# Centring the first half of a weight matrix on three visits of the second attention instead of in the first

## The chip, the cores and the metric

One core of a Trainium2 chip runs the whole program. The metric is the device time of one execution in microseconds (us). Three runs of the kernel before took 1073.25, 1074.12 and 1074.61 us; their median is 1074.12.

## The reference

Attention with a hashed mask (a query sees only keys of its own bucket), then a Fourier mixing block with a residual, a layer norm and a two-layer perceptron. Cut to what matters:

```python
# attention: B, H, S, D = 4, 8, 768, 64; bits of q and k give buckets, mask = same bucket
attn = softmax(where(mask, q @ k.T / sqrt(D), -1e9)) @ v
x = attn.transpose(0, 2, 1, 3).reshape(B, S, H * D)
u = x + real(fft(fft(x, axis=1), axis=2))
un = (u - mean(u, -1)) / sqrt(var(u, -1) + 1e-06)
out = u + maximum(un @ w_ch1, 0.0) @ w_ch2      # w_ch1: 512 x 2048, w_ch2: 2048 x 512
```

The kernel does not subtract the mean of `u` from each row. It subtracts from `w_ch1` the mean of each of its columns, once, which gives the same product: then a constant added to a row of `u` adds nothing. The division by the standard deviation comes after the second layer.

## The kernel before, in words

**Order.** The batch has four items. The second to fourth attentions run beside the mixing block of the item before them. In all attentions a *visit* is one block of 128 keys of one pair of heads: `attention(b)` yields once a visit, 24 times (4 pairs of heads by `NT` = 6 blocks). The first attention (`b` = 0) runs beside the arrival of `w1`, the on-chip copy of `w_ch1` (128 partitions by 4 row blocks by 2048 columns). That part stands in `tc.manual_schedule`: each engine's queue has the order in which the program writes it. From the second attention on, a planner in the tile framework orders each queue by priorities, by when it reckons operands and buffers ready, and by ties that the program gives: `in_turn()` (L683) queues what it encloses behind the last exponential or copy noted for ScalarE and the last operation noted for VectorE (`done_by`), `behind()` (L879) gives matmuls of the attention more priority.

**A visit of the attention** (`n` counts pairs of heads, `c` key blocks). `scores` (L886): on TensorE the mask (L898) and the scores (L909), half by half, into the PSUM tiles `sc`, of which there are two; the exponential `pk` on ScalarE (L922), in one of two buffers. `tally` (L1027): VectorE adds the exponentials up (`acc`, L1041). `finish` (L1003): `values` (L942), 8 matmuls L947, of the visit before; at the last blocks the key sums (`sum`, L957), and `scale` (L963) with copies on ScalarE (L968, L971, L990) and small steps on VectorE (L979 to L997). `prepare(n + 1)` is advanced by one step a visit: transposes (L779), norms on ScalarE (L761), bits by matmul (L812, L838) and thresholds on VectorE (L816 to L828).

**Arrival of w1** (`weights1`, L722). It comes in 16 slices of 128 by 512, as 64-bit numbers, by DMAs on SP's queue (L704), seven ahead; a slice is fetched into a raw buffer after the conversion that empties that buffer. Slice `i` is row block `i % 4` of the column block `i // 4`. `narrow` converts one: VectorE L639, L643, L649; ScalarE L647, L654, L655. The first attention calls the arrival on four visits of five (L1586), one slice a call.

**Means** (`average`, L659, and `centre`, L675). `average(f)` sums the columns of a column block of 512: 8 matmul instructions into the PSUM tile `ws` (L664), a copy to SBUF on ScalarE (`part`, L669), and at its second step the matmul `wm` (L672, 2 instructions), which gives every partition the mean. `centre` subtracts it from the four row blocks on VectorE (L678). The tiles `ws` and `wm` come from `pt` (L520): tag `ps`, two buffers once `roomy` is off, shared with the bits, the key sums and most tiles of the mixing block. Before, the arrival does this for the first two column blocks: one call after the block's last slice the sums, on the call after that the mean and the subtractions, each ahead of that call's slice or between slices. For the last two blocks the sums and means come after the first attention (L1594 to L1599), are copied to SBUF, and are subtracted on visit 2 of the second attention (L1612).

**Beside the second attention** the mixing of item 0 runs (`mix(0)`), with 2 steps ahead of the visits and then enough steps a visit to keep in pace (L1615): `fold` (VectorE, L1122 to L1140), the channel transform (`cs`, L1162), the sequence transform, 4 steps of pairs of PSUM tiles A and B (L1191), which VectorE adds to `x` (L1205), then `mlp7`, a seven-product form of the perceptron. Its first use of `w1` is `quarters(0)` (L1257): sums and differences of quarters of `w1` on VectorE (L1264 to L1267) and writes of blocks of `w1` to DRAM on SP's queue (L1269), from where items 1 to 3 read them back (L1444). By the pace, `quarters(0)` belongs to visit 7.

Of the kernel before, what the change touches and what calls it, by code (L numbers as in the profile page):

```python
# [24 lines left out]
DFF = 4 * DM  # L25
# [5 lines left out]
NDC = DM // P  # L31
GTT = 2
GT = GTT * P
WC = 512
# [451 lines left out]
def _main(  # L486
# [172 lines left out]
    def average(f):  # L659


        ps = pt([P, WC], f"ws{f}")
        for c in range(NDC):
            nc.tensor.matmul(  # L664
                ps[32 * c : 32 * c + 32, :], ones, w1[:, c, f : f + WC],
                start=True, stop=True,
            )
        part = wt([P, WC], F32, "u", f"part{f}", 2)
        nc.scalar.copy(part, ps)  # L669
        yield  # L670
        ps = pt([P, WC], f"wm{f}")
        nc.tensor.matmul(ps, mean, part, start=True, stop=True)  # L672
        yield ps

    def centre(f, avg):  # L675
        for c in range(NDC):
            w = w1[:, c, f : f + WC]
            nc.vector.tensor_tensor(w, w, avg, op=ALU.subtract)  # L678

    ET = mybir.EngineType  # L680
    done_by = {}

    @contextmanager  # L683
    def in_turn():

        with ExitStack() as st:
            for ins in done_by.values():
                st.enter_context(tc.issue_after(ins.ins))
            yield
# [32 lines left out]
    def weights1():  # L722
        slices = [
            (w1[:, c, f : f + WC], moe_w_ch1[c * P : (c + 1) * P, f : f + WC])
            for f in range(0, DFF, WC)
            for c in range(NDC)
        ]
        zt = wt([P, 3, 2 * WC], F32, "z", "zraw1", 1)
        ft = wt([P, 12, WC], F32, "F", "fraw", 1)
        raws = [zt[:, i] for i in range(3)] + [  # L730
            ft[:, i : i + 2].rearrange("p i w -> p (i w)") for i in range(0, 8, 2)
        ]
        arrival = Arrival(slices, raws, 0, nc.sync)
        for i in range(arrival.depth):
            arrival.fetch(i)
            if i == 2:
                load(1)
        yield
        half = None
        for i in range(len(slices)):  # L740
            arrival.convert(i, ft[:, 8 + i % 4].bitcast(I32))
            yield
            if half:
                centre(half[0], next(half[1]))
                half = None
            if i % NDC == NDC - 1:


                f = i // NDC * WC
                if f < DFF // 2:  # L750
                    half = f, average(f)
                    next(half[1])


    xs = {}
# [164 lines left out]
    def weights(pk, g, ps):  # L920

        done_by[ET.Activation] = nc.scalar.activation(  # L922
            pk[:, g, :, 0:HALF], ps[:, :, 0:HALF], AF.Exp, scale=SCALE
        )

    def weigh(n, c, pss):
# [6 lines left out]
        if kb is not None:  # L933
            for h in range(2):
                w = pk[:, :, h, 0:HALF]
                done_by[ET.DVE] = nc.vector.scalar_tensor_tensor(  # L936
                    w, qb[:, h].rearrange("p (g s) -> p g s", g=2), kb[:, h, c : c + 1], w,
# [61 lines left out]
    def attention(b):  # L999
# [14 lines left out]
        for t in range(NPAIR):  # L1014
# [12 lines left out]
            def tally(c, pk, sums):  # L1027
# [10 lines left out]
                else:  # L1038

                    for g in (0, 1) if b == 0 else (slice(0, 2),):  # L1040
                        done_by[ET.DVE] = nc.vector.tensor_tensor(  # L1041
                            acc[:, g], (first if c == 1 else acc)[:, g], new[:, g],
# [102 lines left out]
    def mix(b):  # L1145
# [8 lines left out]
        for par in range(2):  # L1154
            for t in range(NT // 2):
# [12 lines left out]
                for k in kinds:  # L1168
                    done_by[ET.Activation] = nc.scalar.copy(
                        f[:, k, k : hd + 1 - k],  # L1170
# [14 lines left out]
        for j in range(NDC):  # L1185
# [10 lines left out]
            for ps, op in (pa, ALU.add), (pb, ALU.subtract):  # L1196
                for i in range(2):
# [4 lines left out]
                    else:  # L1202
                        f = ps[:, HW : HALF + 1]
                        f = bass.AP(f.tensor, f.offset, [f.ap[0], [HW, 2], [-1, HW]])
                    done_by[ET.DVE] = nc.vector.tensor_tensor(  # L1205
                        u, u, f, op=op if (j < 2) ^ i else ALU.add
# [371 lines left out]
    with tc.manual_schedule(engines={ET.PE, ET.DVE, ET.Activation, ET.Pool, ET.SP}):  # L1578
        for _ in prepare(0):
            pass  # L1580
        roomy[0] = False
        for i, _ in enumerate(attention(0)):
            if i == 2 * NT - 1:
                nc.sync.dma_start(ch, cn["ch"].ap())
                nc.sync.dma_start(sq, cn["sq"].ap())
            if i % 5 < 4:  # L1586
                next(other, None)
        for _ in other:
            pass
        pwf = wt([P, 2, P], F32, "ef", "pwf", 1)  # L1590
        nc.sync.dma_start(pwf, cn["pw"].ap())
        nc.scalar.copy(pw, pwf)
        means = []
        late = [(f, average(f)) for f in range(DFF // 2, DFF, WC)]  # L1594
        for _, avg in late:
            next(avg)
        for f, avg in late:
            means.append((f, wt([P, WC], F32, "u", f"mean{f}", 2)))
            nc.scalar.copy(means[-1][1], next(avg))  # L1599
    for b in range(B):  # L1600
        if b > 0:

            wait = 0
            if b == 1:
                next(other)
                next(other)
                wait = 2
            steps, done = NPAIR * NT - wait, 2 if b == 1 else 0  # L1610
            for i, _ in enumerate(attention(b), 1):
                if b == 1 and i == 2:  # L1612
                    for f, avg in means:
                        centre(f, avg)
                while done * steps < (MIX - LEFT) * (i - wait):  # L1615
                    next(other)
                    done += 1
        if b == B - 1:
            roomy[0] = True

            ms = const.tile([P, 3], F32, tag="ms", name="ms")
            nc.vector.tensor_reduce(ms[:, 0:2], norms, axis=AX.X, op=ALU.max)
            nc.vector.tensor_reduce(ms[:, 2:3], strange, axis=AX.X, op=ALU.max)
            ps = pt([1, 3, P], "norms_t")
            for io in range(3):
                nc.tensor.transpose(ps[:, io, :], ms[:, io : io + 1], ident)
            mt = const.tile([1, 5], F32, tag="mt", name="mt")
            nc.vector.tensor_reduce(mt[:, 0:3], ps, axis=AX.X, op=ALU.max)  # L1630
            nc.vector.tensor_tensor(mt[:, 3:4], mt[:, 0:1], mt[:, 1:2], op=ALU.mult)
            nc.vector.tensor_scalar(
                mt[:, 4:5], mt[:, 3:4], (SAFE / SCALE / 2) ** 2, None, op0=ALU.is_gt
            )
            fl = const.tile([1, 1], I32, tag="fl", name="fl")
            nc.vector.scalar_tensor_tensor(
                fl, mt[:, 2:3], 0.0, mt[:, 4:5], op0=ALU.is_gt, op1=ALU.max
            )
            large = nc.values_load(fl[0:1, 0:1], min_val=0, max_val=1)
        for _ in other:  # L1640
            pass
        other = mix(b)
        if b == 0:
            zt2 = wt([P, 3, 2 * WC], F32, "z", "zraw2", 1)
            arrival2 = weights2()
            other = after(NT, other, islice(arrival2, HF + 2))
# [47 lines left out]
```

## Time and profile before

| what | value |
|---|---|
| median of 3 runs | 1074.12 us |
| the profiled execution | 1074.1 us |
| its span | 1072.3 us |
| TensorE matmul, busy | 1033.3 us (96%) |
| VectorE, busy | 779.6 us (73%) |
| ScalarE, busy | 489.2 us (46%) |
| first attention | from about 13 to 113 us |
| sums, copies, means and subtractions of the first two column blocks | 33.5 to 43.0 us and 58.1 to 66.7 us |
| the same of the last two | 112.6 to 120 us; subtractions 119.7 to 131.3 us |
| writes of w1 to DRAM (24) | 6 from 91.8 us, 18 from 125.2 to 137.8 us |

The profile is of one execution. PE is TensorE, DVE VectorE, ACT ScalarE, POOL GpSimd, SP the queue that issues most DMAs; L664 is line 664 of the kernel. Times are in us from the start of the span. A row of the timeline or of a group gives the engine, the line, the operation, output and inputs by the program's names, and in brackets how long the engine sat idle ahead of it and what ended that. "The chain" is the work that ended last, followed back from the end. Rows by stretch give for each engine the busy time within the stretch and the number of instructions, then TensorE's granted clock, the share of the DMA engines and GB/s.

### The profile page before, as it was taken

Reading aid. Unit: us, or ns where it says so; the run is one execution under the profiler, and the core shown is the slowest. Engines: PE = TensorE matmul, PEld = TensorE weight load, DVE = VectorE, ACT = ScalarE, POOL = GpSimd, SP = SyncE. Lnnn points to the kernel's source line nnn. Section 1 sums busy time; section 2 is a strip of 40 time slices with the busy share of each in tenths; the row PEclk is TensorE's granted clock in tenths of the full one; section 3 lists DMA queues with packets and bytes.
Section 4 is the critical chain, followed back from the end, with each engine's and each line's share of the span. In section 5 each row is a group of like instructions: output and inputs, shape, how many; then the busy total and the mean of one; then the engine's idle time right before and its main releaser. Section 6 shows DMA issues by size and latency. Waiting matters only on the chain.

```text
span 1072.3 us, 14129 instructions
## 1 busy us (share of the span) xinstructions
PE 1033.3 (96%) x4965; PEld 632.4 (59%) x4965; DVE 779.6 (73%) x1326; ACT 489.2 (46%) x993; POOL 59.6 (6%) x132
## 2 busy tenths in 40 slices
PE   7999899999999999999999999999999999999996
PEld 3333364457644676546665675555675579668575
DVE  5789969996799967877758877767857885644353
ACT  7888564761386323455236315354325512440420
POOL 0000000011000020100000020010000012200000
PEclk9999999999999999999999999999999999999999
DMA  8754551470154451223072242322042204223301
GB/s 207 200 143 85 112 136 45 135 233 1 35 153 150 136 194 36 45 67 81 12 200 74 66 123 88 59 64 61 15 125 86 64 25 172 65 74 100 117 20 42
DMA packets 175711, 103.13 MB, mean 96 GB/s; under 512 B 129553, under 2 KB 162961, under 8 KB 175633
## 3 DMA queue, kind: packets, MB, share of 16 engines
q1 hardware_dynamic: 169840, 88.65, 30.7%
q0 software_dynamic: 4224, 13.11, 3.9%
q8 instruction: 41, 0.67, 0.3%
q10 hardware_dynamic: 1568, 0.39, 0.2%
q14 instruction: 38, 0.30, 0.1%
HBM read 81.14 MB, written 20.97 MB: 95 GB/s over the span
## 4 chain that ended last, share of the span: by engine, by line
PE 74%; DVE 14%; ACT 5%; issue 2%; DMA 2%; SPq 1%; DVEq 0%; ACTq 0%
PE o L1350 25%; PE h_p L1471 23%; PE oo L947 9%; PE sc L909 8%; PE cs L1162 3%; DVE pk L936 2%; DVE acc L1041 2%; ACT pk L922 2%; PE A L1191 2%; PE B L1191 1%; PE sum L957 1%; DMA kn<-in_k_dram 1%; DVE x L1205 1%; PE bits L838 1%; SPq L576 1%
## 5 line engine op out<-in xcount | busy, mean ns | idle before, releaser
L1350 PE MATMUL o<-w,h 128*128 128x256 f32 x1152 | 258.6, 381 | 0.9 <-DVE w L1362 0.5
L1350 PEld LDWEIGHTS o<-w,h 128*128 128x128 f32 x1152 | 216.7, 190 | 41.6 <-issue 6.4
L922 ACT ACTIVATE pk<-sc 128x768 f32<-128x768 f32 x192 | 147.4, 808 | 78.6 <-PE oo L947 35.5
L1471 PE MATMUL h_p<-x,w 128*128 128x384 f32 x448 | 164.5, 494 | 2.4 <-ACT w L1538 1.7
L936 DVE SCALAR_TENSOR_TENSOR pk<-qb,kb,pk 128x768 f32<-128x768 bf16 x132 | 128.8, 1012 | 39.4 <-ACT pk L922 39.3
L909 PE MATMUL sc<-qt,kt 64*128 64x384 f32 x768 | 153.6, 503 | 1.6 <-ACT pk L922 1.4
L947 PE MATMUL oo<-pk,vn 128*64 128x385 f32 (+1 forms) x768 | 146.2, 495 | 1.5 <-DVE pk L936 1.3
L1471 PEld LDWEIGHTS h_p<-x,w 128*128 128x128 f32 x448 | 81.9, 190 | 68.3 <-issue 9.3
L1471 PE MATMUL h_p<-w 128*128 128x384 f32 x288 | 105.9, 489 | 0.0
L1041 DVE TENSOR_TENSOR acc<-acc,pk 128x1536 f32<-128x1536 f32 (+1 forms) x64 | 98.5, 1550 | 5.4 <-ACT pk L922 5.2
L947 PEld LDWEIGHTS oo<-pk,vn 128*64 128x64 f32 x768 | 50.5, 136 | 86.5 <-issue 73.7
L909 PEld LDWEIGHTS sc<-qt,kt 64*128 64x128 f32 x768 | 66.2, 186 | 55.4 <-issue 19.3
L1471 PEld LDWEIGHTS h_p<-w 128*128 128x128 f32 x288 | 53.7, 190 | 38.8 <-issue 1.6
L1362 DVE SCALAR_TENSOR_TENSOR w<-o,rs,w 128x256 f32<-128x256 f32 x56 | 26.6, 480 | 41.6 <-PE o L1350 41.6
L1380 ACT COPY tq<-o 128x256 f32<-128x256 f32 x24 | 8.9, 372 | 104.0 <-PE o L1350 104.0
L1485 ACT ACTIVATE h<-h 128x384 f32<-128x384 f32 x72 | 37.4, 524 | 29.0 <-DVE h L1527 14.0
L1350 PE MATMUL o<-w 128*128 128x256 f32 x176 | 42.2, 383 | 0.3 <-DVE w L1362 0.2
L1522 DVE TENSOR_TENSOR h<-h 128x384 f32<-128x384 f32 x32 | 17.8, 555 | 29.2 <-ACT h L1521 29.1
L1100 POOL DMA_DIRECT2D out_dram<-w x30 | 16.3, 546 | 405.4 <-issue 321.4
L1350 PEld LDWEIGHTS o<-w 128*128 128x128 f32 x176 | 32.9, 190 | 7.6 <-DVE w L1362 1.2
L1396 DVE TENSOR_TENSOR tq<-tq,o 128x256 f32<-128x256 f32 x24 | 10.0, 418 | 36.4 <-PE o L1350 36.4
L1369 ACT COPY tq<-o 128x256 f32<-128x256 f32 x24 | 8.8, 368 | 60.3 <-PE o L1350 60.2
(171 smaller groups left out, 1306.0 us busy)
## 6 DMA issues: line engine op xcount, KB each, us to landing
w<-ad SPq DMA_DIRECT2D x168, 128.0 KB, 2.0
w<-bd SPq DMA_DIRECT2D x42, 512.0 KB, 4.5
zraw<-in_moe_w_ch_dram POOLq DMA_DIRECT2D x16, 512.0 KB, 3.9
bd<-w SPq DMA_DIRECT2D x14, 512.0 KB, 4.4
vn<-in_v_dram SPq DMA_DIRECT2D x32, 192.0 KB, 3.3
qn<-in_q_dram SPq DMA_DIRECT2D x120, 48.0 KB, 2.4
kn<-in_k_dram SPq DMA_DIRECT2D x60, 96.0 KB, 3.1
zraw<-in_moe_w_ch_dram SPq DMA_DIRECT2D x8, 512.0 KB, 6.6
```

The costliest lines, as they stand in the source:

```text
L909: last[0] = nc.tensor.matmul(ps[:, h, 0:HALF], kt[rows, ks], qt[rows, qs], start=kb is not None or early, stop=not early,)
L922: done_by[ET.Activation] = nc.scalar.activation(pk[:, g, :, 0:HALF], ps[:, :, 0:HALF], AF.Exp, scale=SCALE)
L936: done_by[ET.DVE] = nc.vector.scalar_tensor_tensor(w, qb[:, h].rearrange("p (g s) -> p g s", g=2), kb[:, h, c : c + 1], w, op0=ALU.is_equa ...
L947: oo = nc.tensor.matmul(oos[g][h * D : (h + 1) * D, 0:w], nat["v", n][:, (2 * c + h) * D : (2 * c + h + 1) * D], pk[:, g, h, 0:w], start=( ...
L1041: done_by[ET.DVE] = nc.vector.tensor_tensor(acc[:, g], (first if c == 1 else acc)[:, g], new[:, g], op=ALU.add,)
L1162: nc.tensor.matmul(ps[:, pc + 2 * lo : pc + 2 * hi - 1 : 2], z[:, cp, pc, par, t * P : (t + 1) * P], ch[:, cp, pc, lo:hi], start=(cp == 0) ...
L1191: nc.tensor.matmul(ps[:, cols], F[:, par, k, t, j * P : (j + 1) * P], sq[:, t, k, cols], start=(t == 0), stop=(t == 1),)
L1350: nc.tensor.matmul(ps, a[:, r], right7[i][:, r], start=start and r == 0, stop=r == HF // 2 - 1, skip_group_check=not start,)
L1362: nc.vector.scalar_tensor_tensor(t[:, cols], src, r, t[:, cols], op0=ALU.mult, op1=ALU.add)
L1471: nc.tensor.matmul(ps, left[:, k], right[i][:, k], start=start and k == 0, stop=k == 1, skip_group_check=not start,)
L1485: done_by[ET.Activation] = nc.scalar.activation(h, h, AF.Relu)
L1522: done_by[ET.DVE] = nc.vector.tensor_tensor(c22, c21, c22, op=ALU.add)
```

## The change

The arrival of `w1` no longer averages and centres anything. A new generator, `centrings`, does the first two column blocks: it lets four visits pass, makes the sums of block 0 on the fifth, its mean and subtractions and the sums of block 1 on the sixth, and the mean and subtractions of block 1 on the seventh. It is called once a visit of the second attention, ahead of that visit's steps of the mixing block, within `in_turn()`. The last two blocks stay as they were.

```diff
+    def centrings(columns, visits):
+
+        for _ in range(visits):
+            yield
+        for f in columns:
+            avg = average(f)
+            next(avg)
+            yield
+            centre(f, next(avg))
+        yield
+
...
-        half = None
         for i in range(len(slices)):
             arrival.convert(i, ft[:, 8 + i % 4].bitcast(I32))
             yield
-            if half:
-                centre(half[0], next(half[1]))
-                half = None
-            if i % NDC == NDC - 1:
-
-
-                f = i // NDC * WC
-                if f < DFF // 2:
-                    half = f, average(f)
-                    next(half[1])
...
+    centred = centrings(range(0, DFF // 2, WC), 4)
     for b in range(B):
...
                 if b == 1 and i == 2:
                     for f, avg in means:
                         centre(f, avg)
+                if b == 1:
+                    with in_turn():
+                        next(centred, None)
                 while done * steps < (MIX - LEFT) * (i - wait):
                     next(other)
                     done += 1
```

## The prediction, made before the result was known

> **What bounds the kernel now.** I read the page's slices first, then the busy time by stretch, then the timeline of the first attention, then the chain of waits.
>
> The slices, of 26.8 us each:
>
> ```profile
> PE   7999899999999999999999999999999999999996
> DVE  5789969996799967877758877767857885644353
> ACT  7888564761386323455236315354325512440420
> ```
>
> TensorE reads as full nearly everywhere, so the share cannot tell which stage is worth what. The busy time by stretch (length, then busy time of each engine) can:
>
> ```profile
> 46.00:58.00 12.00, 8.88 (x62) 3.45 (x58) 11.62 (x16) 8.91 (x17) 0.00 (x0) 1.00 0.66 174
> ...
> 119.00:131.00 12.00, 10.36 (x66) 4.86 (x66) 12.00 (x25) 6.54 (x12) 0.00 (x0) 1.00 0.55 120
> 131.00:166.00 35.00, 35.00 (x214) 21.08 (x213) 24.84 (x36) 19.26 (x39) 1.86 (x3) 1.00 0.52 121
> 166.00:184.00 18.00, 15.93 (x68) 8.18 (x67) 16.93 (x23) 8.72 (x18) 0.53 (x1) 1.00 0.18 59
> ```
>
> The reader is to see three regimes. In the first attention (about 13 to 113 us) VectorE and ScalarE limit and TensorE has holes: 3.1 us in 46 to 58. From 119 to 131 VectorE is full. From 131 to 166, where the visits of the second attention lie to which the change moves work, TensorE has no hole at all: 35.00 of 35.00.
>
> The timeline at the two averages of the first attention (start, length, what, idle time before it and who ended it):
>
> ```profile
> 33.82 1.04 PE L664 MATMUL ws<-w,ones 128*32 128x512 f32 x8
> ...
> 34.93 0.59 ACT L669 COPY part<-ws 128x512 f32<-128x512 f32 x1 [2.30 <-PE ws L664]
> ...
> 39.39 1.13 PE L672 MATMUL wm<-part,mean 128*128 128x512 f32 x2
> ...
> 40.57 2.46 DVE L678 TENSOR_TENSOR w<-w,wm 128x512 f32<-128x512 f32 x4
> ```
>
> ```profile
> 58.10 1.07 PE L664 MATMUL ws<-w,ones 128*32 128x512 f32 x8 [1.94 <-DVE qkb L816]
> ...
> 59.23 0.58 ACT L669 COPY part<-ws 128x512 f32<-128x512 f32 x1 [4.22 <-PE ws L664]
> ...
> 63.05 1.12 PE L672 MATMUL wm<-part,mean 128*128 128x512 f32 x2
> ...
> 64.21 2.48 DVE L678 TENSOR_TENSOR w<-w,wm 128x512 f32<-128x512 f32 x4 [1.81 <-PE wm L672]
> ```
>
> ScalarE stands still 2.30 and 4.22 us ahead of the copies of the sums (L669). The second time TensorE itself waits until VectorE has emptied the PSUM tile of the previous bits (L816). The chain of waits goes through these pieces:
>
> ```profile
> 40.65 2.38 DVE w L678 x4
> ...
> 58.10 1.11 PE ws L664 x8
> 59.21 0.02 issue
> 59.23 0.58 ACT part L669
> ```
>
> **What the Trainium skill says.** "PSUM — Partial Sum Buffer", Engine vs sequencer instructions: the queues of ScalarE and VectorE are strictly first in, first out, and matmuls start and complete in program order. The trace agrees: behind the copy waiting 4.22 us stands the conversion of slice 8 (L647), whose data had landed long before; it starts at 59.72. "Perfetto Trace Analysis", Identifying the Most-Contended Engine: matmul busy share is no good measure of nearness to the roofline. So I use it only where the chain also runs on TensorE; from 131.2 to 165.8 every piece of the chain is TensorE. "VectorE: DVE Perf Modes", Mode 1×: a two-tensor fp32 operation gives one result a cycle, also with a PSUM operand, at 0.96 GHz. For 512 columns that is an estimated 533 ns; the trace has 680 ns from PSUM (wm) and from SBUF (mean) alike, so reading the average in PSUM costs VectorE nothing extra.
>
> **The change, part by part.**
>
> *Removed from the first attention.* Twice: 8 sum matmuls (1.04 and 1.07), a copy (0.59 and 0.58), the averaging matmul (1.13 and 1.12), four subtractions (2.46 and 2.48). TensorE 4.36, ScalarE 1.17, VectorE 4.94 us. What this is worth I get by walking the engines' queues with the same durations.
>
> First average: the exponential of visit 5 ends at 32.63. Without the copy ScalarE does the conversion of slice 4 (0.68+0.69+0.77+0.18, 2.3 with gaps) and reaches the next exponential at 35.1 rather than 37.61; its scores follow the key sums on TensorE at 34.0, so they are there. ScalarE then has 1.5 exponential, 1.2 for the scaling copies and 2.2 conversion: the exponential of visit 7 at 40.0 rather than 42.27. Gain 2.3. VectorE gains more (no subtractions, 2.46), but must wait for that exponential.
>
> Second average: the exponential of visit 10 ends at 55.01, with the 2.3 taken off 52.7. Conversion of slice 8 until 54.9. The scores of visit 11 can follow the bits matmuls on TensorE at about 54.4, so its exponential starts at 55.2 rather than 61.91: gain 6.7. Then TensorE limits: values, key sums and scores (1.5+0.7+0.9) put the next exponential at 59.3 (was 65.45, gain 6.15), and values ahead of the scaling copies the one after at 64.5 (was 70.15). ScalarE is full again from there and the gain stays **5.6 us**. The loads of the fourth head pair shift with it: SP starts them at 63.35 only because its last fetch of w1 waits for the conversion of slice 8 (end 61.82). Bounds: 7.7 if all of both stalls and copies came off (2.30+0.59+4.22+0.58); 4.0 if VectorE, busy 11.62 of 12 us in 46 to 58, holds the walk back.
>
> *Added to the second attention.* The calls at visits 1 to 4 issue nothing. Visit 5 issues 8 sum matmuls and a copy; visit 6 the averaging matmul, four subtractions, then 8 sum matmuls and a copy; visit 7 the averaging matmul and four subtractions. By the scores in the timeline these visits begin near 136, 144 and 150 us. TensorE there has no hole, so its part is on the path: 2 x 1.05 + 2 x 1.12 = **4.3 us**. ScalarE's 1.17 lies in 15.7 us of idle time (131 to 166), VectorE's 4.94 in 10.2 us. If VectorE's cover were gone, its 4.94 would replace TensorE's 4.3, 0.6 more.
>
> *Waits added.* In the second attention the general PSUM tag ("ps") has two buffers. The sum tile holds one until its copy, the average tile one until the fourth subtraction, 2.5 us. Queued behind on TensorE are the pairs A and B (L1191), which need both; scores and values (1.49+1.44 us) have their own tiles and can go first if the planner puts them first. The trace of before shows no such overlap here. Bounds: +2.5 for each of two averages if nothing fits in between, that is +5; and below nothing, -4.0, because the sum matmuls need only w1 and a buffer and may be planned into the holes before and after (119 to 131: 1.64; 166 to 184: 2.07; together 3.7), plus little elsewhere. I take 0, between them: one visit's scores and values are as long as one holding.
>
> *In-turn.* The copies and subtractions stay behind the last noted exponential and accumulation. VectorE is idle from 143.28 to 146.34, so the first subtractions find room; behind the second stand L1205 and the quarters (L1264). Taken at 0, bounds 0 to +1.
>
> *SP and GpSimd.* Of the 24 writes of w1 to DRAM (L1269, 24 x 0.618 us of SP) 16 read the first two column blocks. Before, six went at 91.76 and 18 from 125.16 to 137.8. Now these 16 can go only after the subtractions, past about 150: 16 x 0.62 = 9.9 us of SP among the loads of the last pair of that batch (147.38 to 161.0). SP is then nearly free until 193.6, and the first read back stands at 193.61, so I cost it at nothing; without that cover it is the last rival below. The conversions' fetches on SP come earlier, as walked. GpSimd's queue has none of the moved work and only fetches of the second weight behind other engines: 0.
>
> *Unchanged.* The last two blocks' means and their eight subtractions (119.7 to 131.3).
>
> **Sum.** -5.6 + 4.3 + 0 = -1.3 us. Against the profiled execution (1074.1 us; span 1072.3 and 1.8 around it) that is 1072.8; the median of the runs shown is 1074.12, the same within 0.1, so 1072.8 stands for it too. What this kernel's measurement can tell from no change is about 0.2%, 2.1 us: faster means below 1072.0, slower above 1076.3.
>
> **Rivals.**
> *A, the trade above:* 1072.8, its own range 1072.0 to 1076.3. For it: TensorE's 35.00 of 35.00.
> *B, the added matmuls find cover.* The planner starts sums in TensorE's holes at 119 to 131 and the later ones at 166 to 184 shrink, 3.7 us in all; if half to nearly all of the 4.3 is covered, about 2.2 paid in the middle: 1074.1 - 5.6 + 2.2 = 1070.7. For it: such early issue is seen for loads and norms (the norm of the last keys at 165.95). Against it: cs matmuls ahead of the sums in order want the same buffers.
> *C, the PSUM buffers become the bound.* Place: L1191 at visits 6 and 7. Price: 2.5 us for each average and 1.1 for each sum whose copy is late, 7.2 at most. It decides the sign once over 1.3 + 2.1 = 3.4 us of it is exposed; all exposed gives 1074.1 - 1.3 + 7.2 = 1080.0, in the middle some 1077.5. Against it: scores and values fill.
> *D, SP's writes stand ahead of the last pair's loads* and wait for the subtractions. ScalarE's norm of those queries starts at 158.58, about 3 us after the last load (154.53 + 1.05) is issued, so a delay reaches the exponentials behind it. Price 9.9 less some 5 of slack: 1074.1 - 1.3 + 4.9 = 1077.7.
>
> **Chances.** A 0.42, B 0.41, C 0.12, D 0.05. So faster 0.41, same 0.42, slower 0.17. The range: 1069.0 (B with 0.5 of its cost paid) to 1077.0 (the lower part of C and D) leaves out some 0.05 below and 0.13 above.
>
> **What will show it.** Right: no ws, part or wm before 100 us except the late blocks'; the exponential that was at 70.15 at about 64.5; scores of the second attention's first visit near 110.1 rather than 115.69; TensorE full from about 126 to 165, with 16 sum and 4 averaging instructions more. Wrong: a gain under 4 at the end of the first attention (VectorE held the walk back), holes on TensorE before A and B (C), sums in the holes (B), or a ScalarE norm waiting for a load (D).

## The result and the profile after

The changed kernel takes **1078.06 us** (median of 6 runs, 1077.35 to 1078.51) against 1073.86 us for the kernel before beside it: ratio **1.0035** (95% interval 1.0024 to 1.0045), 3.8 us slower. The prediction was 1072.8 with 1069.0 to 1077.0. The profiled execution took 1077.4 us with a span of 1075.6 us (1072.3 before).

Busy time by stretch, kernel after:

```profile
46.00:58.00 12.00, 11.58 (x85) 4.42 (x84) 11.40 (x21) 11.81 (x21) 0.00 (x0) 1.00 0.43 136
119.00:131.00 12.00, 10.53 (x65) 5.16 (x62) 11.63 (x18) 5.27 (x11) 0.00 (x0) 1.00 0.32 87
131.00:166.00 35.00, 34.37 (x205) 19.48 (x205) 21.52 (x33) 16.79 (x33) 1.86 (x3) 1.00 0.44 109
166.00:184.00 18.00, 13.10 (x58) 6.98 (x57) 16.48 (x28) 7.84 (x16) 0.53 (x1) 1.00 0.39 118
```

The first attention did what was hoped: in 46 to 58 TensorE rose from 8.88 to 11.58 us. From 119 to 131 the hole is as large as before (10.53 of 12), so no added matmul went there. The stretch that got worse is the last: from 166 to 184 TensorE fell from 15.93 to 13.10 us busy. (The same stretch of time holds somewhat different work in the two kernels.)

I use the start of a visit's exponential (L922) as a landmark; visits are counted from 0 through both attentions, so visit 24 is the first of the second attention and visit 30 the first of its second head pair. After minus before, in us (the whole run after lies about 0.3 earlier from its start):

| visit | 7 | 11 | 12 | 13 | 16 | 24 | 28 | 29 | 30 | 31 | 32 | 35 | 95 |
|---|---|---|---|---|---|---|---|---|---|---|---|---|---|
| after | -2.67 | -7.47 | -7.06 | -6.85 | -3.60 | -4.55 | -5.84 | -2.88 | -2.52 | -3.63 | **+4.73** | +4.04 | +3.51 |

Two steps are not those of the prediction. The gain falls by 3.3 between visits 13 and 16, and **8.4 us are lost between visits 31 and 32**, of which 7.7 are left at visit 35. (A visit's start is a place in a planned order, not a sum of costs: e17 below starts visit 32 11.5 us later than the kernel before and visit 35 1.0 us earlier.) TensorE's timeline there, kernel after (start, length, engine, line, output and inputs, count, idle time before and who ended it):

```profile
144.78 1.12 PE L672 MATMUL wm<-part,mean 128*128 128x512 f32 x2
145.84 1.06 PE L664 MATMUL ws<-w,ones 128*32 128x512 f32 x8
146.83 1.56 PE L909 MATMUL sc<-qt,kt 64*128 64x384 f32 x8
148.32 1.51 PE L947 MATMUL oo<-pk,vn 128*64 128x385 f32 x8
149.77 0.92 PE L1191 MATMUL A<-sq,F 128*128 128x193 f32 x4
...
165.60 1.10 PE L672 MATMUL wm<-part,mean 128*128 128x512 f32 x2
166.54 1.47 PE L1191 MATMUL A<-sq,F 128*128 128x193 f32 x8
170.21 1.57 PE L1191 MATMUL B<-sq,F 128*128 128x193 f32 x8 [2.21 <-DVE w L678]
...
173.71 1.61 PE L909 MATMUL sc<-qt,kt 64*128 64x384 f32 x8 [1.60 <-ACT pk L922]
```

At the first average scores and values stand between `wm` and the first A, and TensorE does not wait: so far the prediction's picture. But these pairs A, B now come one visit later than before (149.77, was 147.66), and the second average, made at 165.60, falls behind the sums of the finished head pair (L957, 164.68). In this order only A stands between: the fourth B waits 2.21 us for the subtractions (L678), because the average holds the second PSUM buffer. In the kernel before TensorE goes through these A and B without a wait and waits 0.80 us behind them. The chain of waits shows the rest. First the kernel before, then after (start, length, what):

```profile
164.95 0.83 PE sum L957 x8
...
165.80 0.58 DVE rt L979
166.38 1.64 DVE acc L1041
```

```profile
166.95 0.59 DVE w L678
167.54 0.67 DVE w L652 x2
168.21 0.21 DVE rr L983
168.42 1.73 DVE w L678 x3
170.15 0.52 DVE x L1205 x2
...
171.00 1.75 DVE acc L1041
```

The accumulation (L1041) of the new pair's first two visits starts at 166.31 before and at 171.00 after; it frees the buffers that the exponential of visit 32 writes to (168.12 before, 172.84 after):

```profile
172.84 1.51 ACT L922 ACTIVATE pk<-sc 128x768 f32<-128x768 f32 x2 [2.57 <-DVE acc L1041]
```

The scores behind it wait 1.60 us for that exponential. So two things stand at this place: the held PSUM buffer, and subtractions ahead of the accumulation in VectorE's queue. The average was in its PSUM buffer from 165.60 until 170.16, 4.6 us, since VectorE took its four subtractions in two parts; the first one was held from 144.78 to 148.50, 3.7 us. The prediction had 2.5 us for each.

How much of the loss is TensorE standing still? From the exponential of visit 24 to that of visit 35 the three kernels below do the same matmuls, but for the 20 that are added (and two more of L947 in e17, a run of the next section). Length of that stretch and busy time, for before, after and e17:

```profile
118.17:216.05 97.88, 92.36 (x452) 49.79 (x450) 83.44 (x148) 58.73 (x120) 5.02 (x9) 1.00 0.42 109
113.62:220.09 106.47, 97.65 (x473) 51.28 (x471) 87.75 (x156) 59.65 (x122) 5.02 (x9) 1.00 0.40 107
113.35:215.02 101.67, 96.56 (x475) 51.81 (x475) 87.59 (x156) 59.18 (x121) 5.02 (x9) 0.98 0.42 113
```

TensorE is idle for 5.5 us in it before, 8.8 after and 5.1 in e17.

### The profile page after: what moved, and what is told of

It reads as the page before. It is cut to its first block, busy times and chain, and to the rows that moved or that the text cites. A ratio compares the mean times of both kernels' runs of the same rounds, so it can differ in the third digit from the quotient of the medians.

```text
span 1075.6 us, 14135 instructions
## 1 busy us (share of the span) xinstructions
PE 1034.5 (96%) x4965; PEld 633.3 (59%) x4965; DVE 779.1 (72%) x1326; ACT 489.5 (46%) x993; POOL 59.7 (6%) x132
## 4 chain that ended last, share of the span: by engine, by line
PE 73%; DVE 14%; ACT 7%; issue 3%; DMA 2%; SPq 1%; DVEq 0%; ACTq 0%
PE o L1350 25%; PE h_p L1471 23%; PE oo L947 8%; PE sc L909 8%; ACT pk L922 3%; PE cs L1162 2%; DVE pk L936 2%; PE A L1191 2%; DVE acc L1041 2%; PE B L1191 1%; DVE x L1205 1%; SPq L576 1%; DMA kn<-in_k_dram 1%; PE bits L838 1%; ACT fraw L647 1%
## 5 line engine op out<-in xcount | busy, mean ns | idle before, releaser
L922 ACT ACTIVATE pk<-sc 128x768 f32<-128x768 f32 x192 | 147.3, 808 | 82.5 <-PE oo L947 35.6
L936 DVE SCALAR_TENSOR_TENSOR pk<-qb,kb,pk 128x768 f32<-128x768 bf16 x132 | 128.8, 1012 | 40.7 <-ACT pk L922 39.6
L947 PE MATMUL oo<-pk,vn 128*64 128x385 f32 (+1 forms) x768 | 146.2, 495 | 1.3 <-DVE pk L936 1.1
L1041 DVE TENSOR_TENSOR acc<-acc,pk 128x1536 f32<-128x1536 f32 (+1 forms) x64 | 98.5, 1550 | 5.3 <-ACT pk L922 5.1
L947 PEld LDWEIGHTS oo<-pk,vn 128*64 128x64 f32 x768 | 50.5, 136 | 86.7 <-issue 73.9
```

The lines of the kernel that those rows point to most:

```text
L922: done_by[ET.Activation] = nc.scalar.activation(pk[:, g, :, 0:HALF], ps[:, :, 0:HALF], AF.Exp, scale=SCALE)
L936: done_by[ET.DVE] = nc.vector.scalar_tensor_tensor(w, qb[:, h].rearrange("p (g s) -> p g s", g=2), kb[:, h, c : c + 1], w, op0=ALU.is_equa ...
L947: oo = nc.tensor.matmul(oos[g][h * D : (h + 1) * D, 0:w], nat["v", n][:, (2 * c + h) * D : (2 * c + h + 1) * D], pk[:, g, h, 0:w], start=( ...
L1041: done_by[ET.DVE] = nc.vector.tensor_tensor(acc[:, g], (first if c == 1 else acc)[:, g], new[:, g], op=ALU.add,)
```

## The experiments

All against the kernel before on the same chip; "us" is the ratio's distance from 1 times 1074.

| run | what differs from the kernel after | median us | ratio (95%) | us | clock |
|---|---|---|---|---|---|
| after | | 1078.06 | 1.0035 (1.0024 to 1.0045) | +3.8 | 0.997 |
| e1_none | first two blocks not centred | 1068.55 | 0.9943 (0.9930 to 0.9955) | -6.1 | 0.998 |
| e2_sums_only | no subtractions | 1073.35 | 0.9989 (0.9983 to 0.9996) | -1.2 | 0.998 |
| e3_sbuf_mean | average copied to SBUF by ScalarE | 1073.88 | 0.9994 (0.9986 to 1.0002) | -0.6 | 0.997 |
| e5_hold | the same, PSUM buffer held | 1075.82 | 1.0018 (1.0010 to 1.0025) | +1.9 | 0.998 |
| e17_vector_copy | average copied by VectorE | **1072.84** | **0.9984 (0.9977 to 0.9991)** | **-1.7** | 0.996 |
| e9_visit_earlier | one visit earlier | 1077.38 | 1.0027 (1.0018 to 1.0037) | +2.9 | 0.997 |
| e11_sbuf_earlier | earlier, copied by ScalarE | 1080.07 | 1.0040 (1.0026 to 1.0054) | +4.3 | 0.996 |
| e18_vector_copy_earlier | earlier, copied by VectorE | 1074.28 | 0.9998 (0.9989 to 1.0007) | -0.2 | 0.998 |
| e6_first_only | only the first block moved | 1073.59 | 0.9998 (0.9990 to 1.0007) | -0.2 | 0.998 |
| e10_first_only_sbuf | the same, copied by ScalarE | 1076.61 | 1.0021 (1.0013 to 1.0028) | +2.3 | 0.997 |
| e7_all_means_early | averages between the attentions | 1073.30 | 0.9995 (0.9987 to 1.0004) | -0.5 | 0.998 |
| e4_late_tables | two table loads later | 1078.34 | 1.0036 (1.0024 to 1.0048) | +3.9 | 0.994 |
| e12_earlier_late_tables | e9 and e4 together | 1076.82 | 1.0016 (1.0007 to 1.0024) | +1.7 | 0.996 |
| e8_before_late_tables | kernel **before**, tables later | 1073.69 | 0.9998 (0.9988 to 1.0008) | -0.2 | 0.997 |
| e15_copy_a_slice_later | kernel **before**, averages in later steps | 1076.01 | 1.0012 (1.0006 to 1.0019) | +1.3 | 0.996 |
| e16_copy_later_late_tables | e15 and e8 together | 1075.40 | 1.0015 (1.0007 to 1.0023) | +1.6 | 0.996 |

The last column is TensorE's granted clock, as a share of full speed, averaged over the runs of that kernel. It matters, because 0.001 of it is about 1.1 us. In nine of the traces it fell to 0.50 for 3.41 us at some place between 20 and 1060 us (e9, e11, e13, e14, e16 and e17 once, e12 and e15 twice, in e4 once for 6.83 us). Each 3.41 us takes up to 1.7 us of TensorE's work. The traces of before, after, e1, e2, e3, e5 to e8, e10 and e18 have no such stretch. The times show it too: of the 36 runs of the kernel before beside e1 to e4, the 25 with a clock of 0.997 or more have a median of 1073.49, the other 11 one of 1075.97. So a difference of some 2 us between kernels of unlike clock may be the clock. Where a reading hangs on it, the text below gives the median of the runs at 0.997 or more, called "at full clock".

### What the addition costs

**e1_none**

```diff
-    centred = centrings(range(0, DFF // 2, WC), 4)
+    centred = iter(())
```

> The changed kernel without the centring of the first two column blocks at all (that part of the computation is left out). Theory: removal gains 4.3 in the first attention and the added work costs about 8.1 in the second, so without it 1078.1 - 8.1 = 1070.0. Rival 'the planner's other order of everything behind is to blame, not the added work': little falls away, 1075 or more.

Measured 1068.55. The removal alone is worth 6.1 us by the ratio, 5.5 by the medians, 5.1 in the trace (visit 95) and 4.9 at full clock, about the 5.6 of the prediction. All that was added costs 9.9 us by the ratios (9.1 at full clock), not 4.3.

**e2_sums_only**

```diff
-            centre(f, next(avg))
+            next(avg)
```

> The changed kernel with sums, copies and averaging matmuls in place, but the eight subtractions left out (so the first two column blocks are not centred). Theory (4.4 us of TensorE work, and 3.7 from the subtractions: they hold a PSUM buffer ahead of A and B and stand in VectorE's chain): 1078.1 - 3.7 = 1074.4. Rival 'the matmuls alone, by their place in TensorE's queue, cost all 8': 1078. Rival 'writes of w1 on SP wait for the subtractions': the writes are free here, so also about 1074; the next run tells it from the theory.

Measured 1073.35. Sums, copies and averaging matmuls cost 4.9 us over e1 (predicted 4.3 for TensorE), and the subtractions 4.9 more. As VectorE's work, as holders of PSUM, or by the order that is planned around them? In this run the first A, B also follow their sums at once, not a visit later.

### Is it the PSUM buffer?

**e3_sbuf_mean**

```diff
-            centre(f, next(avg))
+            m = wt([P, WC], F32, "u", f"mean{f}", 2)
+            nc.scalar.copy(m, next(avg))
+            centre(f, m)
```

> The changed kernel with each average copied from PSUM to SBUF by ScalarE (2 x 0.6 us) and subtracted from there, so that the PSUM buffer is free after the copy. Theory in the form 'the held PSUM buffer': B does not wait its 2.2 us and the second average can come a visit earlier, 1074.4 to 1076. Theory in the form 'the subtractions in VectorE's chain': unchanged, 1077 to 1078.5. Rival SP: unchanged, 1078.

Measured 1073.88: 4.4 us better than after, with the same subtractions on VectorE. So the 4.9 us of VectorE's work are not the cost by themselves. The release of the buffer is earlier here, but the order is another too: at the end of the pair the accumulation (168.48) now stands ahead of the subtractions (170.19). And TensorE still waits 2.52 us ahead of the first A, for ScalarE's copy.

**e5_hold** puts the holding back. It is e3, and behind the subtractions one column of the PSUM tile is read by VectorE (0.16 us).

```diff
             centre(f, m)
+            nc.vector.tensor_copy(m[:, 0:1], ps[:, 0:1])
```

> The changed kernel with each average copied to SBUF by ScalarE and subtracted from there, as in e3_sbuf_mean, but with one tiny VectorE read of the PSUM tile (one column) put behind the four subtractions, so that the tile is again held until they are done. VectorE's added work is two instructions of well under 0.1 us each. If holding one of the two PSUM buffers through the subtractions is what costs the 4 us, the time goes back to about 1078 (1077 to 1079) and TensorE again does a visit's scores before the first pair A and B. If e3 was faster for another reason (the source of the subtraction, or ScalarE's share in the work), it stays near 1074.

Measured 1075.82: 2.6 us of the 4.4 come back, not all. The first tile is now held from 144.63 to 151.89, longer than in the kernel after, and the first B waits 1.41 us for its last read. At the end of the pair the planned order does two visits' scores (171.14 and 174.35) ahead of the last B; they wait 1.54 and 1.59 us for exponentials. So holding costs something here as well, but its length alone is not its price: what is put under it counts.

**e13_dve_copy and e14_dve_copy_earlier** were to copy by VectorE. The kernels that ran did not contain that edit: by their traces the copy (L689) is on ScalarE, and their instructions are those of e3 and e11.

> As e3_sbuf_mean, but VectorE, not ScalarE, copies the average to SBUF, right ahead of its own four subtractions. In e3 the copy stood in ScalarE's queue behind a conversion that waited for its data, and TensorE waited 2.52 us for it ahead of the first A. If the lateness of the buffer's release is what costs, that wait shrinks to about 1 us: 1072 to 1073, in spite of 1.3 us more VectorE work. If e3 was faster only because the second average left the end of the pair, it stays at 1074 or rises with VectorE's work to 1075.

> e9_visit_earlier with the average copied to SBUF by VectorE. e9 (held through four subtractions) took 1077.4 and e11 (copied by ScalarE, whose copy waited in its queue until 4 us after the average was made) 1080.1. If the time of release of the PSUM buffer decides, this one, with the release some 0.7 us after VectorE reaches it, is the fastest of the three by 3 us or more: 1073 to 1074.5. If it is the place of the work (subtractions in these visits, sums earlier), it is 1077 or more like the other two.

They count as repeats: 1074.08 (ratio 0.9999, 0.9990 to 1.0007) for e3, and 1077.74 (1.0038, 1.0025 to 1.0051) for e11. The intervals overlap with those of the first time. By the medians e14 is 2.3 us below e11, which the clock can explain (0.997 in e14, 0.996 in e11).

**e17_vector_copy** is e3 with the copy made by VectorE.

```diff
-            nc.scalar.copy(m, next(avg))
+            nc.vector.tensor_scalar(m, next(avg), 1.0, None, op0=ALU.mult)
```

> The changed kernel with VectorE taking the average out of PSUM (a multiplication by 1.0) right ahead of its four subtractions, which read SBUF. The buffer is free 0.7 instead of 2.5 us after VectorE reaches it, and nothing hangs on ScalarE's queue. The planned order is that of the changed kernel up to the fourth pair A, B. If the length of the holding is the cost, the waits of TensorE for the subtractions (2.21 us at the fourth B) fall under 0.5 us: 1074 to 1075.5 with 1.3 us more VectorE work. If the order of VectorE's queue at the end of the pair is the cost (subtractions ahead of the accumulation), holding or not, it stays at 1077.5 to 1079.5.

Measured **1072.84**, faster than both kernels and below what was expected. By the ratios it is 5.5 us better than the changed kernel (4.8 at full clock), with 1.4 us more work on VectorE. TensorE at the same place:

```profile
165.34 1.10 PE L672 MATMUL wm<-part,mean 128*128 128x512 f32 x2
166.27 1.47 PE L1193 MATMUL A<-sq,F 128*128 128x193 f32 x8
167.57 1.47 PE L1193 MATMUL B<-sq,F 128*128 128x193 f32 x8
171.57 0.52 PE L1219 MATMUL un<-ident,x 128*128 128x128 f32 x3 [2.53 <-DVE x L1207]
```

The fourth B follows its A without a wait. Each average is held 1.9 us (144.51 to 146.45 and 165.34 to 167.28). But TensorE then waits 2.53 us for an addition (L1207) that VectorE does behind the subtractions (168.06 to 170.49). So the direct wait of 2.21 us has moved rather than gone. What e17 does not have are the three waits that follow in the kernel after: 1.60 us for the exponential, 1.09 for the masked exponentials (L936) and 1.71 for ScalarE (L1538); the kernel before has the last two as well (1.27 and 1.72). Its plan is another: transposes and mixing matmuls (L1219, L1473) come ahead of the next scores, and the accumulation is put off to 176.22. TensorE is busy 15.15 us in 166 to 184 (13.10 after), some of it at half clock (3.41 us from 172.3). So reading the average out early is worth about 5 us here, and by the traces most of that comes through the order that could then be planned, not through the one wait at the buffer.

### Is it the end of the pair?

**e9_visit_earlier**

```diff
-    centred = centrings(range(0, DFF // 2, WC), 4)
+    centred = centrings(range(0, DFF // 2, WC), 3)
```

> The changed kernel with its three visits taken one visit earlier (the constant 4 is 3). In the planned order the second average then stands ahead of the first pair A, B and no longer behind the sums of the pair's end. Both averages are still held in PSUM through four subtractions. If the cost is that the second average falls at the end of the head pair (B of the fourth tile waits for its buffer, and the subtractions stand ahead of the accumulation for which the next exponential waits), it goes: 1078.1 minus some 3.7, so 1074 to 1075. If a held buffer costs some 2 us wherever it stands, the time stays at 1077 to 1079.

Measured 1077.38. The theory of the pair's end fell: the second average now comes ahead of the first A, and the loss between visits 31 and 32 is gone (+3.50 and +3.50), but between visits 28 and 31 it lost 9.2 us (-5.69 to +3.50). With one buffer held until 149.82 the plan makes both A tiles' halves first, then a visit's scores and values, then B; and the next B waits:

```profile
156.60 2.45 PE L1191 MATMUL B<-sq,F 128*128 128x193 f32 x8 [2.34 <-DVE x L1205]
```

It waits for an addition (L1205) that stands in VectorE's queue behind an operation that waits for ScalarE; and ScalarE's queue waits for fetched data (3.62 and 1.55 us ahead of two conversions). Some 1.7 us of the 9.2 are the clock: from 157.1 it is 0.50 for 3.41 us, and these 8 matmuls take 2.45 us where e18 below needs 1.47, the 8 of the next scores 2.29 against 1.56.

**e11_sbuf_earlier** adds e3's edit to e9.

> The two cures together: one visit earlier as in e9_visit_earlier, and the average subtracted from SBUF as in e3_sbuf_mean. If both take away the same cost (the second average at the end of the pair), they don't add: 1073.5 to 1074.5, about as each alone. If the held buffer costs 1 us or more also in the middle of a pair, it is that much below e9_visit_earlier, 1072.5 to 1073.

Measured 1080.07, a miss: worse than both e3 and e9. The second average is made at 148.03 and freed at 153.07, since ScalarE's copy stands behind two conversions whose data are late; TensorE waits 3.08 us for it. Its trace has half clock for 3.41 us right behind that wait. At full clock its median is 1076.95 (4 of 12 runs), e9's 1076.63 (16 of 22). So ScalarE's copy gained nothing here; that it costs more than the holding is not shown.

**e18_vector_copy_earlier** is e11 with VectorE's copy.

> e9_visit_earlier with the same VectorE copy. e9 (1077.4) waited 2.34 us on TensorE at the second B, behind a chain through VectorE and ScalarE; e11 and e14 (the same program, copy on ScalarE) waited 3.1 us. If the length of the holding is the cost: TensorE's waits between 147 and 160 us fall under 1 us and the time to 1073.5 to 1075. If the place of the work is: 1077 to 1078.5.

Measured 1074.28: by the ratios 3.1 us better than e9 and 4.5 better than e11, at full clock 2.4 and 2.7, with the same work at the same visits and 1.4 us more on VectorE than e9. TensorE at its second average:

```profile
146.14 1.13 PE L672 MATMUL wm<-part,mean 128*128 128x512 f32 x2
147.10 1.47 PE L1193 MATMUL A<-sq,F 128*128 128x193 f32 x8
148.41 1.47 PE L1193 MATMUL B<-sq,F 128*128 128x193 f32 x8
```

No wait. So at both places an early release takes most of the cost away: by the ratios e17 is 4.4 us above e1 and e18 5.9, against 9.9 of the kernel after and 9.0 of e9.

**e6_first_only** leaves the second block in the arrival as it was before the change.

```diff
+            if i == 2 * NDC - 1:
+                half = WC, average(WC)
...
-    centred = centrings(range(0, DFF // 2, WC), 4)
+    centred = centrings(range(0, WC, WC), 4)
```

> Only the first block is averaged and centred in the second attention; the second block is averaged and centred in the first attention, as before the change. Half the added TensorE work (2.2 us) comes with it, and the stall of the first attention at visit 11 stays, so of the gain only the 2.3 to 2.9 us of visit 6 can remain. If each holding of the PSUM buffer costs about 2 us: 1074.0 - 2.5 + 2.4 + 2.1 = 1076. If it is the second holding alone (the 2.5 us ahead of the fourth B) that costs: 1074.0 - 2.5 + 2.4 = 1073.9. If the gain at visit 6 is not kept through the second stall: 2.5 more in each case.

Measured 1073.59, nearest to the expectation in which only the second holding costs. Its gain of 3.3 us at visit 24 is spent by visit 32 (-0.19), of which 2.2 is TensorE.

**e10_first_only_sbuf** adds e3's edit to e6.

> As e6_first_only (only the first block moved), with the average copied to SBUF by ScalarE and subtracted from there, so that the PSUM buffer is free after the copy. In e6_first_only the gain of 3.3 us at the end of the first attention was spent in the second with only 2.2 us of added TensorE work, so 1.1 was left for the holding. If that is the holding, 1072.5 to 1073. If not, the same as e6_first_only, 1073.6.

Measured 1076.61: 2.5 us slower than e6, where a gain was expected. The copy comes at 149.90, behind conversions that waited 2.03 and 1.04 us for data. The tile is held 4.4 us instead of the 3.7 of e6:

```profile
150.61 0.89 PE L1201 MATMUL B<-sq,F 128*128 128x193 f32 x4 [2.45 <-ACT mean L690]
```

**e7_all_means_early** makes all four averages between the attentions and copies them to SBUF, so that only the subtractions are left on the visits.

```diff
-    centred = centrings(range(0, DFF // 2, WC), 4)
+    early = []
+    for first, to in ((0, early), (DFF // 2, means)):
+        late = [(f, average(f)) for f in range(first, first + DFF // 2, WC)]
...
+    centred = centrings(early, 4)
```

> The averages of all four blocks are made between the two attentions and copied to SBUF; on two visits of the second attention only the subtractions of the first two blocks are left, reading SBUF. No PSUM buffer is held. From the run without the first two blocks' centring (1068.6): plus 4.4 of TensorE, of which up to 1.6 finds the holes between the attentions, and nothing for the subtractions: 1071.4 to 1073. If the subtractions cost VectorE time of their own in the second attention whatever they read, up to 4.9 more: 1074 to 1077.

Measured 1073.30. The subtractions at 138.97 and 144.88 us, on the visits where e9 has them, cost little: e7 is 5.6 us above e1 by the ratios, and the averages between the attentions take 4.4 of it at once (the exponential goes from -6.98 at visit 24 to -2.60 at visit 25). Some 1.2 are left, about the width of the intervals. No hole hid the matmuls.

### What became of the gain in the first attention

**e4_late_tables**

```diff
-            if i == 2 * NT - 1:
+            if i == 3 * NT - 1:
```

> The changed kernel with the loads of ch and sq (1.3 MB) issued one head pair later, so that they do not stand ahead of the loads of the fourth pair's queries and keys. Theory: the gain of 6.6 at visit 13 is cut to 4.2 at visit 24 by those loads (waits of 1.6, 1.4 and 2.3 us for them); it should come back by 2 to 3 us, 1075 to 1076. Rival 'the first attention has another bound there': unchanged, 1078.

Measured 1078.34, a miss. In the kernel after, SP (start, length of the group, count) and ScalarE show why the gain sinks from visit 13 to 16:

```profile
58.42 1.40 SPq L1584 DMA_DIRECT2D ch<-k_ch  x1
...
60.34 8.85 SPq L576 DMA_DIRECT2D qn<-in_q_dram  x8
```

```profile
70.95 0.84 ACT L761 ACTIVATE sq<-qn 128x768 bf16<-128x768 f32 x1 [1.59 <-DMA qn<-in_q_dram]
...
74.71 0.84 ACT L761 ACTIVATE sq<-kn 128x768 bf16<-128x768 f32 x1 [1.43 <-DMA kn<-in_k_dram]
```

The loads of the fourth pair start 3.0 us earlier than before but take 8.85 us on the queue instead of 7.82, and with the visits 6.9 us earlier they are now late. In e4 they are not: the gain is 6.73 at visit 24 instead of 4.55. By visit 32 it is +3.06, by visit 95 +4.37. In part this is the clock. In e4's trace it is 0.50 for 6.83 us from 169.9:

```profile
170.00:176.00 6.00, 4.75 (x17) 2.51 (x15) 6.00 (x11) 3.30 (x5) 0.00 (x0) 0.50 0.86 271
```

That can take up to 3.4 us, and the six runs of e4 have a clock of 0.994 on average, those of the kernel after 0.997. In the trace e4's lead over the kernel after goes from 1.7 us at visit 31 to 0.7 at visit 35; it is -0.9 at visit 48, for reasons that the runs don't show. So e4 does not show what the late tables are worth at an equal clock.

**e8_before_late_tables** is the same edit in the kernel before; **e12_earlier_late_tables** is the edit in e9.

> The kernel before, with nothing changed but the issue of the two tables' loads, one head pair later (as in e4_late_tables). In the changed kernel this kept 2.2 us of the first attention's gain up to visit 24 and lost it later. If late loads of the fourth head pair held the kernel before too, it gains up to 1 us in the first attention; if they bind only once the visits come earlier, it is the same up to visit 24 within 0.3 us. At the end: 1074 within 1.

> e9_visit_earlier with the two tables' loads issued one head pair later, as in e4_late_tables. In e4 the late tables kept 6.7 instead of 4.5 us of gain up to the end of the first attention and the second attention then took it back. If that was because the end of the pair set the time whatever came before, then with the end of the pair free the 2.2 us are kept: 1072 to 1072.5. If the second attention takes them back all the same, it is equal to e9_visit_earlier within 0.5.

e8 moved nothing (1073.69): these loads bind only once the visits come earlier. e12 is 1.2 us below e9 with overlapping intervals, and its trace has two stretches of half clock where e9's has one, so that stays open.

**e15_copy_a_slice_later** is the kernel before with each of the first two averages' copy, and then the averaging matmul, one slice later.

```diff
         nc.tensor.matmul(...)
+        if f < DFF // 2:
+            yield
         part = wt([P, WC], F32, "u", f"part{f}", 2)
...
-                centre(half[0], next(half[1]))
-                half = None
+                ps = next(half[1])
+                if ps is not None:
+                    centre(half[0], ps)
+                    half = None
```

> The kernel before, with all averages where they were, except that ScalarE's copy of the sums of the first two blocks is issued one slice after the sum matmuls, and the averaging matmul and the subtractions one slice after that. TensorE's 4.4 us stay in the first attention, where it has holes, and nothing is added to the second. If the stalls of ScalarE (2.30 and 4.22 us ahead of the two copies) are what the change won in the first attention, 4 to 6 us of it come without the cost: 1068 to 1070. If the planned order puts the copies at the same places, or TensorE's work itself was the cost, it stays within 1 us of 1074.

Measured 1076.01, a miss with the other sign. ScalarE no longer waits for the sums, but TensorE does, and the scores behind them in its queue with it. Timeline of e15, TensorE and then ScalarE (L820 there is L816 of the kernel before, L926 is L922):

```profile
58.62 1.07 PE L664 MATMUL ws<-w,ones 128*32 128x512 f32 x8 [3.00 <-DVE qkb L820]
```

```profile
61.42 0.81 ACT L926 ACTIVATE pk<-sc 128x768 f32<-128x768 f32 x1 [4.78 <-PE sc L913]
```

The sums wait for a buffer of the same PSUM tag, which VectorE has yet to empty of the bits. The stall in the kernel before had the same root (L664 there waits 1.94 us for the bits): a wait for a buffer of this tag, the kind that the change put in elsewhere. That nothing was gained is shown; the loss of 1.3 us may be the clock, which is 0.50 for 3.41 us from 59.7 and again from 206.5.

**e16_copy_later_late_tables** is e15 with e8's edit.

> e15_copy_a_slice_later with the two tables' loads issued one head pair later. If e15 gains over 4 us at the middle of the first attention, the loads of the fourth head pair bind as in the changed kernel and this keeps up to 2.2 us more: 1067 to 1069. If e15 gains under 3 us, the two are equal within 0.5 us.

Measured 1075.40, equal to e15 within the intervals, as expected where e15 gains nothing.

## Why the prediction was wrong, point by point

- **Removed from the first attention, 5.6 us: right in sum.** Net of the 0.3 at the start the walk's steps came out as 2.4 (2.3 predicted) at visit 7, 7.2 (6.7) at visit 11, 6.8 (6.15) at visit 12 and 6.6 (5.6) at visit 13; e1 gives 4.9 to 6.1. That the sum fits is in part luck: the walk came out 1.0 too low at visit 13, and it left out a loss. "Stays 5.6" was wrong: the walk moved the fourth pair's loads along with the rest and did not ask whether they then arrive. They were late by 1.59 and 1.43 us, and about 4.3 reached the second attention.
- **Added to TensorE, 4.3 us: right.** e2 minus e1 is 4.9; e17 minus e1, 0.41%, is 4.4. In 119 to 131 TensorE kept its hole, so rival B did not happen.
- **Waits of the PSUM tag, taken as 0: this step failed.** Reading the average out early is worth 5.5 us by the ratios at the change's own place (after minus e17; 4.8 at full clock) and 3.1 one visit earlier (e9 minus e18; 2.4 at full clock). The upper bound in the text was 5. The assumption was that "one visit's scores and values are as long as one holding". Three things in it were wrong. The holding was 3.7 and 4.6 us, not 2.5: it starts with the matmul, and VectorE comes to the subtractions when its queue lets it. The second average did not fall in the middle of a visit but behind the sums of a finished pair, where no scores are ready. And the term counted only waits at the buffer: of these the trace has one for the average, of 2.21 us, and one of 0.55 us at the key sums (L957) that e17 has too. The rest came as other waits in the order planned around the held buffer, as the kernel after, e5 and e9 show.
- **In-turn and VectorE's 4.94 us, taken as 0: right where the average is copied out (e17), open in the kernel after.** e17 minus e1 is 4.4, no more than TensorE's added work, and e7 leaves about 1.2 for the subtractions. In the kernel after they delay the accumulation and with it the exponential and the scores. e17 has them at the same place and is faster, but it does not need the accumulation so soon. How much of the failed term is this delay was not measured.
- **Rivals.** The outcome is that of C, at 1078.06 against 1077.5 for its middle, with its place at L1191; it had been given 0.12 for the reason that scores and values fill. D did not happen: ScalarE's norm of the last queries waited 1.11 us for data after the change and 1.81 us in the faster e17.
- **Sum.** By the ratios: -6.1 + 4.4 + 5.5 = +3.8. (These are differences between runs, so they add up by construction.) e17, in which the third term is about 0, took 1072.84; the prediction for that case was 1072.8. That they agree to a tenth is luck, since e17 has copies and a stretch of half clock that the prediction did not have.

That in-order queues pass a wait on, which the prediction cites from the Trainium skill ("PSUM — Partial Sum Buffer", Engine vs sequencer instructions), decided three runs: e10, e11 and e15. A copy or a matmul was "early" in the program and late in its queue, by 0.9 to 2.8 us behind late data in e10 and e11, by 3.00 us behind an evacuation in e15.

**Still open:** whether another planned order would pay less for the same holding (e5 held longest and paid less than the kernel after), so how far the 5.5 us are a property of this planner's choice; what late tables would be worth at the end of e4 at full clock; and what starts the stretches of half clock.

## What to carry to other kernels

When work is moved that passes through a PSUM tag of few buffers, cost the time from the matmul that fills a buffer to the last reader's end, with the reader's queue in it, and look at what the matmul engine has to do under it at each place, the ends of pairs above all. If several instructions read one PSUM tile, a copy to SBUF ahead of them on the engine that reads next can be worth more than its time (here 1.4 us of VectorE for about 5 us), while the same copy on another engine is only as early as that engine's queue. A stretch that is gained puts later transfers on trial: ask which load has to be there at the new time. And look at the granted clock before a difference of 1 or 2 us is explained by the edit.

## What the runs showed of the hardware

VectorE's multiplication by 1.0 of 128x512 fp32 from PSUM to SBUF took 0.68 us, as long as the two-operand subtraction of that size (0.68); ScalarE's copy of the same tile took 0.57 to 0.59. So ScalarE's is the shorter one, and it was still the worse choice by 1.1 us (e3 against e17) and by 2.7 at full clock (e11 against e18), where it stood in its queue behind conversions whose data were late.

Eleven stretches of half clock stand in these traces between 20 and 1060 us. Ten begin within 1.4 us of the end of a TensorE wait of 2.2 to 3.2 us; the other (e15, 206.5) follows a wait of 1.72 us. But waits of 2.21 us (after), 2.45 (e10) and 2.52 (e3) had none behind them. e3 and e13 are the same program, and one trace has a stretch and the other has not. So in these runs a wait of TensorE could cost up to 1.7 us more than its own length, and not each time.
